# A kernel of attention and gated mixing: the fourth pair of spatial weights loaded earlier, and tiles placed at multiples of 512 bytes

## The chip, the core and the metric

The kernel runs on one core of a Trainium2 chip. A core has five engines that run their own instruction streams and meet through semaphores: TensorE (matrix products, PE in the profile, its weight loads PEld), VectorE (DVE), ScalarE (ACT), GpSimd (POOL) and SyncE (SP), which here only issues transfers. ScalarE and GpSimd issue transfers too. All transfers run on the core's 16 DMA engines. SBUF is the working memory, 128 partitions wide; PSUM holds the results of matrix products.

The metric is device time in microseconds (us) of one execution; lower is better.

## The reference: what is computed

The input x has 2048 tokens of 512 numbers. After a layer norm, two branches read the same xn, and their results are added to x.

```python
x = A_x
xn = _layernorm(x, axis=-1)
return x + _A_ref(xn, A_wqkv, A_wo) + _B_ref(xn, B_w_in, B_w_sp, B_b_sp, B_w_out)
```

Branch A is attention over a sliding window: 32 heads of 16 numbers, each token looks at itself and at the tokens 2, 4, ... 14 before it (8 taps).

```python
logits = jnp.einsum('bhsd,bhswd->bhsw', q, kg) * scale
logits = jnp.where(mask[None, None, :, :], logits, -1000000000.0)
attn = _softmax(logits, axis=-1)
o = jnp.einsum('bhsw,bhswd->bhsd', attn, vg)
```

Branch B is a gated mixing over tokens. z has 1376 columns; the second half is normalised, mixed over all tokens by the 2048 x 2048 matrix w_sp (the spatial weights), and gates the first half.

```python
z = _gelu(jnp.einsum('bsd,df->bsf', x, w_in))
z1 = z[..., :Fh].copy()
z2 = _layernorm(z[..., Fh:], axis=-1)
g = jnp.einsum('ts,bsf->btf', w_sp, z2) + b_sp[None, :, None]
return jnp.einsum('bsf,fd->bsd', z1 * g, w_out)
```

## The kernel before

Tokens are cut into 16 tiles of 128. Everything stays in SBUF: `xnT` holds the normalised tokens transposed, `wts` all input weights (and later the output weights in the same place), `qk0` and `qk1` the queries and keys of the two halves of the tokens, `z2` and `z1` the halves of z, `prod0` and `prod1` products, `vp` the values with a halo of 16 columns, `a_sb` the logits and weights of the attention, `wsp1` and `wsp2` three buffers for the spatial weights. All come from one pool with one buffer each, laid out in SBUF in the order in which they are declared.

The work runs in this order. First the 16 tiles of x are normalised on VectorE, transposed, and multiplied with the weights of z2 (line 225), of queries and keys (265), and then of z1 (225 again). Then come the head sums of the logits (315), the values (280) and the mixing. At the end the output products (423, 437, 450) are added up in PSUM, x is added, and the result is stored.

The mixing is 16 steps M0 to M15 on TensorE (`mix_tile`, line 384), each 32 products of 344 columns: one tile of output tokens against all 16 tiles of z2. Two steps share one load of spatial weights: `load_wsp(n)` (W0 to W7, lines 373 to 377) brings 256 rows of w_sp, transposed on the way, into buffer n modulo 3. W3 thus goes into the buffer of W0, which M0 and M1 read; M6 and M7 use W3. M4 and M5 use W2, M8 and M9 use W4, M10 and M11 use W5. ScalarE moves each result from PSUM to SBUF with the bias (line 387), VectorE multiplies it with z1 (`gate`, g0 to g15, line 392), and SP transposes the product back into `qk0` or `qk1` (line 394).

Beside that, VectorE does the attention. For each half of the tokens (0 and 1): the maximum and its subtraction (x0, x1; lines 325 to 329), ScalarE's exponential (333), the sums (u0, u1; 338 to 340), ScalarE's reciprocal by logarithm and exponential (344, 345), the scaling (c0, c1; 349), and then twelve operations of the taps (a0.0 to a0.11 and a1.0 to a1.11; multiplications line 357, additions 361, the last one 370). Taps from a0.1 on read the halo of V, which GpSimd copies between partitions (lines 286, 287). F0 and F1 are VectorE's last additions of x to the results in PSUM (lines 455, 462); Q0 to Q4 are the output products.

The order of each engine is written out by hand in two lists: `ten` for TensorE with the ScalarE work that belongs to it, `vec` for VectorE. A name in a list emits its instructions, with their transfers on the queue of the engine that issues them. W0, W4 and those after it stand in `ten`. W1, W2 and W3 stand in `vec`, for a reason in the code: `load_wsp` first writes two elements of the buffer on VectorE, so that the transfer follows that memset.

```python
if n in (1, 2, 3):
    V.memset(wsp[n % 3][:, 0, 0:2], 0.0)
SP.dma_start_transpose(wsp[n % 3], B_w_sp[n * 2 * P:(n + 1) * 2 * P, :])
```

The memset of W3 waits until TensorE has finished M1, and SP's transfer waits for the memset. SP issues its transfers in the order of the program: before the change g0's transpose, g1's, W3, g2's, W4, W5.

Of the kernel before, what the change touches and what calls it, by code (L numbers as in the profile page):

```python
# [7 lines left out]
BF16 = mybir.dt.bfloat16  # L8
F32 = mybir.dt.float32
# [4 lines left out]
P = 128  # L14
S = 2048
D = 512
NT = S // P
# [21 lines left out]
def kernel(  # L39
# [22 lines left out]
    sb = ctx.enter_context(tc.tile_pool(name="sb", bufs=1))  # L62
# [17 lines left out]
    b_col = sb.tile([P, NT], F32, name="b_col")  # L80
    stmp = sb.tile([P, 4, GS], F32, name="stmp")

    xnT_r = sb.tile([P, C * S], BF16, name="xnT")
    xnT = xnT_r[:].rearrange("p (c s) -> p c s", c=C)
    op = xnT_r[:].rearrange("p (t d s) -> p t d s", t=2, d=DH)
    wts = sb.tile([P, C * (3 * D + F)], BF16, name="wts")
    w_q, w_k, w_v = [wts[:, C * (FH + n * D):C * (FH + (n + 1) * D)].rearrange("p (k f) -> p k f", k=C) for n in range(3)]

    w_z1 = wts[:, 0:C * FH].rearrange("p (k f) -> p k f", k=C)
# [380 lines left out]
    for i in range(5, NT):  # L470
# [2 lines left out]
    vec = front.split() + """  # L473
        zs0 LW m00 zn0 zn1 zn2 zn3 j00 f00 p00 K m01 d01 m02 d02 zs4 m03 d03 zn4 zn5 zn6 zn7
        p01 p02 zs8 m10 d10 zn8 zn9 zn10 zn11 p03 W1 zs12 m11 zn12 zn13 zn14 zn15 f11 p11 p10 m12 d12
        m13 f13 x0 p13 p12 W2 u0 g0 c0 x1 a0.0 u1 a0.1 g1 W3 c1 a0.2 g2 a0.3 g3
        a0.4 g4 a0.5 g5 a0.6 a0.7 g6 a0.8 g7 a0.9 a0.10 g8 a0.11 g9
        a1.0 a1.1 g10 a1.2 a1.3 g11 a1.4 g12 X1 a1.5 a1.6 g13 a1.7 g14 a1.8 g15 a1.9 a1.10 a1.11 F0 F1
    """.split()
# [278 lines left out]
```

## Time and profile before

| | us |
|---|---|
| median of 3 runs | 201.83 |
| lowest and highest run | 201.72, 201.90 |
| the profiled execution | 201.34 |
| its span (first to last instruction) | 199.6 |
| TensorE busy in it | 194.4 |
| VectorE busy in it | 176.9 |
| ScalarE busy in it | 89.2 |

The profiled execution is one run of its own, 0.49 us below the median; 1.74 us of it lie outside the span. The granted TensorE clock is full speed throughout. In the profile a row of instructions has its line in the kernel, engine, operation, the tiles it writes and reads, and a count; "idle before" is the time in which the engine stood still ahead of them, with what ended it. A row of the timeline begins with its start and its length in us; rows on SPq and POOL that name a DMA show the issue of a transfer, not its length. The chain of waits goes backwards from the last instruction to whatever released each step.

### The profile page before, as it was taken

The page shows a single profiled execution, that of the slowest core. Times are in us where ns is not written, and L with a number is a line of the kernel's source. Part 1 is how long each engine was busy: PE and PEld are TensorE (multiplying, and loading weights), DVE is VectorE, ACT ScalarE, POOL GpSimd, SP SyncE. Part 2 cuts the span into 40 slices and gives each one's busy share as a digit, 9 for nine tenths or more (in the row PEclk, how much of TensorE's full clock was granted, in tenths as well). Part 3 has the DMA queues.
Part 4 walks back from the last instruction along what each step waited for, and adds up shares of the span by engine and source line. Part 5 has one row for each costly group of instructions (what it writes and reads, how often), then busy time and mean ns, then how long its engine had stood idle before and what let it go on. Part 6 is the DMA issues. An engine that isn't in the chain of part 4 may idle for free.

```text
span 199.6 us, 3847 instructions
## 1 busy us (share of the span) xinstructions
PE 194.4 (97%) x1580; PEld 117.9 (59%) x1586; DVE 176.9 (89%) x194; ACT 89.2 (45%) x145; POOL 40.1 (20%) x67
## 2 busy tenths in 40 slices
PE   7999999999999999999999989999999999999993
PEld 2655555655666666666666656666666664444442
DVE  4799789999997999998999999999999999964263
ACT  3868879899888674978531111111112210000000
POOL 4267540138374103000700000011010000000000
PEclk9999999999999999999999999999999999999999
DMA  5999579699959905509808999999999937414033
GB/s 174 295 246 193 106 158 275 120 196 198 198 100 141 208 0 112 107 0 148 124 20 99 234 271 223 231 257 166 255 207 91 267 75 221 84 57 165 0 105 105
DMA packets 64610, 31.09 MB, mean 156 GB/s; under 512 B 53456, under 2 KB 62800, under 8 KB 64464
## 3 DMA queue, kind: packets, MB, share of 16 engines
q1 hardware_dynamic: 59136, 19.24, 48.8%
q0 software_dynamic: 2192, 6.75, 18.0%
q10 hardware_dynamic: 3264, 4.86, 9.5%
q8 instruction: 12, 0.20, 0.4%
q14 instruction: 6, 0.05, 0.1%
HBM read 10.13 MB, written 2.10 MB: 61 GB/s over the span
## 4 chain that ended last, share of the span: by engine, by line
PE 89%; DMA 6%; DVE 3%; issue 1%; POOL 0%
PE mm L384 33%; PE mm L225 18%; PE mm L265 14%; PE mm L280 7%; PE mm L450 7%; PE mm L423 7%; DMA wsp<-in_B_w_sp_dram 5%; PE aux L423 2%; DVE stats L189 1%; DMA z<-in_A_x_dram 1%; PE aux L315 1%; PE mm L437 1%; DVE z L206 1%; DVE mv L190 0%; POOL rstd L197 0%
## 5 line engine op out<-in xcount | busy, mean ns | idle before, releaser
L384 PE MATMUL mm<-z,wsp 128*128 128x344 bf16 x512 | 75.2, 309 | 0.6 <-DMA wsp<-in_B_w_sp_dram 0.6
L384 PEld LDWEIGHTS <-wsp 128*128 128x128 bf16 x512 | 49.9, 98 | 25.7 <-issue 1.3
L225 PE MATMUL mm<-wts,xnT 128*128 128x344 bf16 x256 | 39.5, 309 | 0.1
L387 ACT ACTIVATE qk<-mm,b_col 128x688 bf16<-128x688 f32 x16 | 13.3, 834 | 56.6 <-PE mm L384 52.8
L357 DVE TENSOR_TENSOR prod<-vp,a_sb 128x4096 bf16<-128x4096 bf16 x16 | 36.3, 2285 | 0.0
L225 PEld LDWEIGHTS <-xnT 128*128 128x128 bf16 x256 | 24.7, 98 | 13.7 <-DVE xnT L215 0.4
L301 DVE TENSOR_TENSOR prod<-qk 128x4096 bf16<-128x4096 bf16 (+1 forms) x16 | 31.6, 2020 | 1.2 <-ACT qk L267 1.1
L265 PE MATMUL mm<-xnT,wts 128*128 128x512 bf16 x124 | 28.7, 379 | 0.2
L361 DVE TENSOR_TENSOR prod<-prod,prod 128x8192 bf16<-128x8192 bf16 x6 | 26.5, 4422 | 0.1
L265 PEld LDWEIGHTS <-wts 128*128 128x128 bf16 x128 | 14.6, 114 | 11.9
L267 ACT CAST qk<-mm 128x1024 bf16<-128x1024 f32 x16 | 16.2, 1012 | 4.8 <-PE mm L265 3.8
L280 PE MATMUL mm<-xnT,wts 128*32 128x512 bf16 x256 | 14.5, 379 | 0.0
L450 PE MATMUL mm<-wts,xnT 32*128 32x512 bf16 x192 | 14.3, 374 | 0.0
L423 PE MATMUL mm<-wts,qk 128*128 128x512 bf16 (+1 forms) x63 | 14.0, 370 | 0.2 <-issue 0.2
L257 ACT ACTIVATE z<-mm 128x688 bf16<-128x688 f32 x16 | 11.9, 742 | 4.4 <-PE mm L225 4.4
L423 PEld LDWEIGHTS <-qk 128*128 128x128 bf16 x85 | 8.2, 98 | 9.2 <-issue 0.4
L189 DVE BATCH_NORM_STATS2 stats<-z 128x6 f32<-128x512 bf16 x16 | 11.0, 685 | 2.2 <-DMA z<-in_A_x_dram 2.2
L236 ACT ACTIVATE z<-mm 128x688 bf16<-128x688 f32 x16 | 11.9, 743 | 2.2 <-PE mm L225 2.1
L445 POOL DMA_DIRECT2D qk<-qk x6 | 3.0, 502 | 47.0 <-DMA qk<-z 47.0
L241 ACT ACTIVATE z_junk<-z 128x688 bf16<-128x688 bf16 x16 | 12.3, 771 | 0.0
L280 PEld LDWEIGHTS <-wts 128*32 128x32 bf16 x256 | 9.5, 138 | 4.4
L310 POOL DMA_DIRECT2D prod<-prod x8 | 7.1, 882 | 24.9 <-DVE prod L301 24.9
(97 smaller groups left out, 178.7 us busy)
## 6 DMA issues: line engine op xcount, KB each, us to landing
prod<-prod POOLq DMA_DIRECT2D x8, 512.0 KB, 5.8
wts<-in_A_wo_dram ACTq DMA_DIRECT2D x4, 512.0 KB, 7.0
out_dram<-z SPq DMA_DIRECT2D x9, 128.0 KB, 1.7
z<-in_A_x_dram SPq DMA_DIRECT2D x4, 256.0 KB, 5.1
wts<-in_A_wqkv_dram SPq DMA_DIRECT2D x2, 512.0 KB, 6.6
wsp<-wsp POOLq DMA_DIRECT2D x2, 512.0 KB, 6.2
wsp<-in_A_x_dram ACTq DMA_DIRECT2D x1, 1024.0 KB, 5.8
wsp<-in_A_x_dram SPq DMA_DIRECT2D x1, 1024.0 KB, 6.1
```

The source lines that it names most:

```text
L189: V.bn_stats(stats[:, i, :], xs[:, i, :])
L225: PE.matmul(pz[:, hh, 0:FHALF], xnT[:, kc, i * P:(i + 1) * P], w_z2[:, hh, kc] if part else w_z1[:, kc, hh * FHALF:(hh + 1) * FHALF], star ...
L265: PE.matmul(pq[:, cc, :], w_c[:, kc], xnT[:, kc, t0:t0 + D], start=(kc == 0), stop=(kc == C - 1))
L267: A.copy(qk[b // 2][:, a, 2 * c2:2 * c2 + 2, o:o + D], pq[:])
L280: PE.matmul(pv[32 * g:32 * g + 32, dd, :], w, r, start=(kc == 0), stop=(kc == C - 1), tile_position=(0, 32 * g))
L301: ops.append(lambda ww=ww, k=k, c=c: V.tensor_tensor(pr[:, ww, c], q[:, c], k[:, c], ALU.mult))
L357: return lambda: V.tensor_tensor(dst, vp[:, :, th, off:off + GS], a_sb[:, th, w].unsqueeze(1).broadcast_to([P, DH, GS]), ALU.mult)
L361: return lambda: V.tensor_tensor(dst, dst, x, ALU.add)
L384: PE.matmul(pg[:, hh, 0:FHALF], w[:, k, (j % 2) * P:(j % 2 + 1) * P], z2[:, k, hh * FHALF:(hh + 1) * FHALF], start=(k == 0), stop=(k == NT ...
L387: A.activation(g.rearrange("p (a b) -> p a b", a=2), pg[:, :, 0:FHALF], ACT.Identity, bias=b_col[:, j:j + 1])
L423: PE.matmul(po[:, cols], uT[th][:, m, t0:t0 + P], wout[:, m, cols], start=(start and m == 0), stop=(stop and m == MF - 1))
L450: PE.matmul(po[tiles[g]], op[32 * g:32 * g + 32, th, d, s * P:(s + 1) * P], wo_r[32 * g:32 * g + 32, d, :], start=False, stop=(tiles[g] in ...
```

## The change

Two things are changed. In the list `vec`, W3 moves from behind g1 to behind x1, ahead of the tap a0.0: so its memset stands earlier on VectorE, and its transfer stands ahead of g1's transpose on SP. And two tiles are declared that nothing reads or writes, `pad0` of 64 bytes per partition ahead of `xnT`, `pad1` of 256 ahead of `qk0`. They move all that follows in SBUF, so that `xnT`, `wts`, `qk0`, `wB`, `prod0`, `prod1`, `z2`, `z1`, `vp`, `a_sb`, `wsp1` and `wsp2` begin at multiples of 512 bytes. All engines execute the same instructions as before.

```diff
@@ -80,10 +80,13 @@
     b_col = sb.tile([P, NT], F32, name="b_col")
     stmp = sb.tile([P, 4, GS], F32, name="stmp")
 
+    sb.tile([P, NT], F32, name="pad0")
+
     xnT_r = sb.tile([P, C * S], BF16, name="xnT")
     xnT = xnT_r[:].rearrange("p (c s) -> p c s", c=C)
     op = xnT_r[:].rearrange("p (t d s) -> p t d s", t=2, d=DH)
     wts = sb.tile([P, C * (3 * D + F)], BF16, name="wts")
+    sb.tile([P, 2 * D // 8], BF16, name="pad1")
...
@@ -473,7 +476,7 @@
     vec = front.split() + """
...
-        m13 f13 x0 p13 p12 W2 u0 g0 c0 x1 a0.0 u1 a0.1 g1 W3 c1 a0.2 g2 a0.3 g3
+        m13 f13 x0 p13 p12 W2 u0 g0 c0 x1 W3 a0.0 u1 a0.1 g1 c1 a0.2 g2 a0.3 g3
```

## The prediction

> **What bounds the kernel now.** I read the page's busy shares first, then the chain of waits, then TensorE's own waits, then the timeline around the one wait that is left.
>
> ```profile
> span 199.6 us, 3847 instructions
> PE 194.4 (97%) x1580; PEld 117.9 (59%) x1586; DVE 176.9 (89%) x194; ACT 89.2 (45%) x145; POOL 40.1 (20%) x67
> ```
>
> TensorE is busy for all but 5.2 us of the span, most of that at the two ends. Its waits between 9 and 197 us:
>
> ```profile
> PE mm L384 <- DMA wsp<-in_B_w_sp_dram: 0.6, 1, 0.6
> PE mm L423 <- issue: 0.2, 1, 0.2
> ```
>
> So one data wait is left inside, and the chain of waits says whose it is:
>
> ```profile
> 92.67 13.97 PE mm L384 x96
> 106.65 9.96 DMA wsp<-in_B_w_sp_dram
> 116.61 0.14 issue
> 116.74 8.33 PE mm L384 x56
> ```
>
> The 9.96 us are not lost: the chain follows the load back to its issue, while TensorE went on with M4 and M5. The loss is on the timeline:
>
> ```profile
> 92.61 23.51 PE L384 MATMUL mm<-z,wsp 128*128 128x344 bf16 x160
> 96.35 1.23 DVE L329 TENSOR_TENSOR a_sb<-a_sb,stmp 128x2048 bf16<-128x2048 bf16 x1
> 97.49 0.83 ACT L387 ACTIVATE qk<-mm,b_col 128x688 bf16<-128x688 f32 x1 [2.09 <-PE mm L384]
> 102.48 2.28 DVE L357 TENSOR_TENSOR prod<-vp,a_sb 128x4096 bf16<-128x4096 bf16 x1
> 105.14 0.06 DVE L376 MEMSET wsp<- 128x1 uint32 x1
> 106.65 5.54 SPq L377 DMA_TRANSPOSE wsp<-in_B_w_sp_dram  x1
> 116.74 8.47 PE L384 MATMUL mm<-z,wsp 128*128 128x344 bf16 x57 [0.62 <-DMA wsp<-in_B_w_sp_dram]
> ```
>
> M1 to M5 run without a gap from 92.61 to 116.12; M6 needs W3, which lands at 116.61, and starts at 116.74. The gap is 0.62 us. W3 could have come sooner: its buffer is that of M0 and M1, and M1's eviction begins at 97.49. W3 was held by its memset, which stands behind g1 on VectorE (105.14).
>
> **The move of W3.** On VectorE the memset (0.06) passes six instructions: the tap a0.0, the three sums u1, the tap a0.1 and the gate g1. It now follows L329, which ends at 96.35 + 1.23 = 97.58. It waits for M1, seen finished by ScalarE at 97.49, so VectorE should not stand still. On SP, W3's transpose passes one transfer, g1's. No DMA is added; the queues of POOL and ACT keep their order.
>
> W3 is then issued at about 97.7 (SP is free: g0's transpose went out at 93.72 and one takes 1.2). The eight such loads took 7.6 to 10.0 us to land, so W3 is there between 105.3 and 107.7. M6 can start at 116.12, 8.4 us later at least. The 0.62 us go; the 0.14 of "issue" lie inside them.
>
> Behind W3 on SP stands g1's transpose. SP needs 4.2 to 7.1 us to issue a load, so it is free by 104.8; g1's gate ends at 104.68 + 0.51 = 105.19. No delay. Then g2's transpose (gate ends at 110.03), then W4 at about 111.4 instead of 113.63. It meets the output weights that ACT loads from 111.55, as W3 did before; with W3's slow landing (10.0) it is there at 121.4, and M8 wants it at 116.12 + 2 x 4.67 = 125.5. W5 waits for M5 to leave its buffer (116.1), is issued near 116.5 and lands by 126.5; M10 wants it near 134.8. So no later load becomes the wait.
>
> What starts earlier beside other work: POOL's two copies of V's halo (issued 95.69 and 97.14, 5.3 and 4.1 us to landing) are down at 101.24, and tap a0.1 reads them at 102.48, a slack of 1.24. W2's data began to move 1.5 us after its issue, so W3's begins at 99.2 and overlaps the halo for 2.0 us. From below: no delay, since the busy share of the DMA engines is 0.89 from 98 to 99 us, 0.70 in the next and 0.39 in the one after, so most of the halo is through when W3 comes. From above: the halo behind all of W3 (a rival, below). The nearest row is a small POOL transfer issued beside W3 in this trace: 5.7 us to landing, against 5.1 and 4.8 for the two other such copies of 8 KB, so 0.6 to 0.9 longer. I take that: the halo at 101.9 to 102.1, still in time, cost zero. If this cover goes, each us of stall shifts VectorE by one, and then this slack counts:
>
> ```profile
> DVE wsp L575 <- PE aux L450: 5.3, 1, 5.3
> DVE z L462 <- PE mm L450: 1.5, 1, 1.5
> ```
>
> The second wait is F0 before its first result: 1.48 now, 0.86 when TensorE is 0.62 earlier. F0's four additions end at 179.16 and TensorE takes their banks again at 180.09, 0.93 later. VectorE may therefore lose 0.86 + 0.93 = 1.79 us before TensorE feels it.
>
> **The new addresses.** pad0 (64 bytes) and pad1 (256) shift what follows. From the tiles' sizes, xnT and wts began 448 bytes past a multiple of 512, qk0, wB, prod, z2, z1, vp, a_sb and wsp 192 past; now 0, but for qk1 (256). No instruction is added. For the compute engines the trace prices this: z2 is read at steps of 688 bytes, hence at many offsets, and the 512 matmuls of L384 last 306 to 320 ns; L357 reads vp at a start that moves 4 bytes per tap, 2284 to 2286 ns; ScalarE writes z2 at steps of 1376 bytes (L236) and z1 at 1536 (L257), median 744 for both. Zero, within 14 ns of an instruction.
>
> For DMA the trace has no pair of like transfers at two offsets. Only two places on the path can feel it. One is the first load of x (0.80 to 3.04), which holds the front. The fastest transfer of that size is a store of 1.7 us, so at best 2.24 - 1.7 = 0.5 is gained. The other is the load of tokens 4 and 5, issued at 4.41, 5.0 us; VectorE waits 0.37 us for it, and the copy of transposed tile 3 that TensorE needs next (C3) is queued behind that wait. The slowest of that size took 6.3, so at worst 1.3 is lost; at best 0.04, TensorE's gap there. I take zero, as the engines' rows show no offset that matters, and keep -0.5 and +1.3 for the range.
>
> [...]
>
> **Sum.** The profiled execution took 201.34 us (span 199.6 and 1.74 around it): 201.34 - 0.62 = 200.72. It ran 0.49 below the median of the three runs, 201.83; on that, 201.83 - 0.62 = 201.2.
>
> **Rivals.**
> A second gain, from the addresses. For it: two SBUF ends of transfers lie on the path. Against: nothing in the trace shows an offset's price. Half of the 0.5 bound besides the move: 200.9.
>
> The wait moves on. VectorE, late by 1.8 to 2.4 us for the halo, gives most of it back at Q2; or some later transfer is late. Against: the margins above (8.4, 4.0, 1.79). About 201.7. That the change does not bring W3 forward belongs here: it would need the memset held until g1 anyway, against M1's end at 97.49.
>
> Slower, by the halo. If W3's 1 MB goes ahead of it on the 16 engines, the halo comes with W3, at 97.6 + 7.6 = 105.2 at the earliest; a0.1 stalls 2.7 us, TensorE is late by 2.7 - 1.79 = 0.9 at Q2, net +0.3: 202.1 (with a landing of 10.0, 204.5). It decides from a stall of 2.41. For it: W loads run near 290 GB/s and leave the engines full. Against: the halo starts moving about 1 us ahead of W3, and the 0.6 to 0.9 above. [...]
>
> Slower, by the front: the second load 1.3 us later, 202.5. For it only that bound.
>
> **How the numbers follow.** About 0.2% (0.4 us) is what a measurement of this kernel can tell from no change, so "faster" ends at 201.43. Forecast (201.2): 0.60, of which 0.04 falls short of 201.43 since 0.62 is only 0.22 beyond it. Second gain (200.9): 0.12. Wait moves on (201.7): 0.16. Halo (202.1 and up): 0.08. Front (202.5): 0.04. Faster 0.56 + 0.12 = 0.68; same 0.16 + 0.04 = 0.20; slower 0.12. The range goes down to 200.6 (the move with the whole 0.5 is 200.7, and the runs spread 0.1) and up to 202.1, the halo's nearer price.
>
> **What would show it.** Right: W3's memset near 97.6 and its issue right behind, no wait of L384 on the weights, M6 at 116.1, a0.1 near 102.5, F0's wait near 0.9, every matmul and VectorE row unchanged within 14 ns, x's first load at 2.2. Wrong: a VectorE wait on the vp DMA before a0.1 (halo); a wait at L384 in M8 or M10; Q2 waiting for VectorE; a first load of x well off 2.24, or a start of the L225 work that moved.

## The result

The changed kernel took 200.45 us (median of 6 runs, 200.33 to 200.62). The kernel before, run beside it, had a median of 201.78 (4 of 6 runs); the ratio is 0.9938 (95% interval 0.9923 to 0.9953). That is faster by 0.6%, about twice the 0.3% forecast, and 200.45 lies 0.15 us below the low end of the range. In a later comparison, on another chip, the same two kernels gave 0.997 (0.9952 to 0.9987): the two put the gain at 0.6 and 0.3%. Some executions, of the kernel before above all, take 203 to 217 us; the ratios and the medians leave them out, and "4 of 6" says how many of all are counted.

The page after, its first lines:

```profile
span 198.7 us, 3847 instructions
PE 194.0 (98%) x1580; PEld 117.7 (59%) x1586; DVE 176.9 (89%) x194; ACT 89.3 (45%) x145; POOL 40.1 (20%) x67
```

The profiled execution took 200.43 us, 0.91 less than the one of before. TensorE's waits between 9 and 197 us are now these:

```profile
PE mm L426 <- issue: 0.2, 1, 0.2
```

The wait for the spatial weights is gone. (Three lines were added to the file, so line 384 is now 387, and so on.) The timeline around it, after:

```profile
92.49 34.74 PE L387 MATMUL mm<-z,wsp 128*128 128x344 bf16 x237
96.26 1.23 DVE L332 TENSOR_TENSOR a_sb<-a_sb,stmp 128x2048 bf16<-128x2048 bf16 x1
97.37 0.83 ACT L390 ACTIVATE qk<-mm,b_col 128x688 bf16<-128x688 f32 x1 [2.07 <-PE mm L387]
97.43 0.06 DVE L379 MEMSET wsp<- 128x1 uint32 x1
97.59 6.33 SPq L380 DMA_TRANSPOSE wsp<-in_B_w_sp_dram  x1
102.77 2.29 DVE L360 TENSOR_TENSOR prod<-vp,a_sb 128x4096 bf16<-128x4096 bf16 x1 [0.32 <-DMA vp<-vp]
116.04 0.83 ACT L390 ACTIVATE qk<-mm,b_col 128x688 bf16<-128x688 f32 x1 [3.83 <-PE mm L387]
120.71 0.83 ACT L390 ACTIVATE qk<-mm,b_col 128x688 bf16<-128x688 f32 x1 [3.83 <-PE mm L387]
```

The memset runs at 97.43 and W3 goes out at 97.59. TensorE has one row of 237 products, up to the end of this view, where it had 160, a gap, and the next row. M5's result is evicted at 116.04 and M6's at 120.71, 4.67 us later, which is one step of the mixing.

Where the 0.91 come from, by these evictions. Before, the last two rows of the same kind are

```profile
116.15 0.83 ACT L387 ACTIVATE qk<-mm,b_col 128x688 bf16<-128x688 f32 x1 [3.83 <-DMA wts<-in_B_w_out_dram]
121.60 0.83 ACT L387 ACTIVATE qk<-mm,b_col 128x688 bf16<-128x688 f32 x1 [4.62 <-PE mm L384]
```

M5 came 0.11 us earlier after the change and M6 0.89. So 0.78 were won at M6 and 0.11 in the front; M15's result is 0.89 ahead as well (163.60 and 162.71), and nothing is given back up to the end.

The slack of VectorE, after:

```profile
DVE wsp L578 <- PE aux L453: 5.3, 1, 5.3
DVE z L465 <- PE mm L453: 0.3, 1, 0.3
```

F0 now waits 0.31 us in place of 1.48.

### The profile page after: what moved, and what is told of

It is laid out like the page before. It is cut to its first block, busy times and chain, and to the rows that moved or that the text cites. A ratio compares the mean times of both kernels' runs of the same rounds, so it can differ in the third digit from the quotient of the medians.

```text
span 198.7 us, 3847 instructions
## 1 busy us (share of the span) xinstructions
PE 194.0 (98%) x1580; PEld 117.7 (59%) x1586; DVE 176.9 (89%) x194; ACT 89.3 (45%) x145; POOL 40.1 (20%) x67
## 4 chain that ended last, share of the span: by engine, by line
PE 94%; DVE 3%; DMA 1%; issue 0%; POOL 0%
PE mm L387 38%; PE mm L228 18%; PE mm L268 14%; PE mm L283 7%; PE mm L453 7%; PE mm L426 7%; PE aux L426 2%; DVE stats L192 1%; DMA z<-in_A_x_dram 1%; PE aux L318 1%; PE mm L440 1%; DVE z L209 1%; DVE mv L193 0%; POOL rstd L200 0%; DVE z L586 0%
## 5 line engine op out<-in xcount | busy, mean ns | idle before, releaser
L270 ACT CAST qk<-mm 128x1024 bf16<-128x1024 f32 x16 | 16.2, 1013 | 4.7 <-PE mm L268 3.7
L283 PE MATMUL mm<-xnT,wts 128*32 128x512 bf16 x256 | 14.5, 379 | 0.0
L244 ACT ACTIVATE z_junk<-z 128x688 bf16<-128x688 bf16 x16 | 12.4, 772 | 0.0
```

What stands on the lines that cost most here:

```text
L270: A.copy(qk[b // 2][:, a, 2 * c2:2 * c2 + 2, o:o + D], pq[:])
L283: PE.matmul(pv[32 * g:32 * g + 32, dd, :], w, r, start=(kc == 0), stop=(kc == C - 1), tile_position=(0, 32 * g))
```

## The experiments

A job is a set of kernels run by turns on one chip. The kernel before, over four jobs: 201.5 (32 of 88).

**The move alone**, twice, the second time on the same chip as the whole change.

```diff
-   ... a0.0 u1 a0.1 g1 W3 c1 a0.2 ...
+   ... W3 a0.0 u1 a0.1 g1 c1 a0.2 ...      (no pads)
```

> W3 behind x1, no pads: the move alone. Theory A (two independent gains): the wait at M6 goes and is worth 0.78 us, which is what M6's eviction moved against M5's between the two traces (121.60 - 116.15 = 5.45 before, 120.71 - 116.04 = 4.67 after); the front stays as before (first product of line 265 near 12.3 in the trace, the load of tokens 4 and 5 at 5.0 us). Time 0.996 of before. Theory B (the move is all, and its wait is longer in most executions than in the profiled one): the time is that of the whole change, 0.994. Theory C (the addresses are all: aligned loads land sooner, W3 among them): 0.999 to 1.0. By A and B VectorE still waits about 0.3 us for the halo of V.

> The move without the pads, beside the whole change on the same chip. If the addresses are worth nothing, the undisturbed executions of the two lie within 0.1% of each other, around 200.4, and both have few executions over 203. If they are worth something, this is 0.1 to 0.3% slower and has more of them (3 of 12 in the first run, against 1 of 30 in the kernels with W3 early and pads).

> The whole change again: 200.3 to 200.6, no wait at L384, M5 and M6 evicted 4.67 us apart, and at most one execution of twelve over 203; against the kernel before, whose undisturbed executions lie between 200.2 and 202 as W3's landing takes 7.5 to 10 us or more, a ratio of 0.994 to 0.997.

Measured: 200.61 (9 of 12), ratio 0.9977 (0.9937 to 1.0016); then 200.50 (12 of 12), ratio 0.9963 (0.9941 to 0.9986), beside 200.36 (7 of 8) and 0.997 for the whole change. The trace of the first has no wait at line 384; M5 and M6 are evicted at 116.21 and 120.87, 4.66 apart. The first interval includes 1 and tells little; the second does not, and there the move alone and the whole change have one time within 0.07%, less than the measurement tells. So the move alone gives the gain, as theory B has it. VectorE waited 0.56 us for the halo here, and 0.89 in the second trace of this kernel.

```profile
103.18 2.29 DVE L357 TENSOR_TENSOR prod<-vp,a_sb 128x4096 bf16<-128x4096 bf16 x1 [0.56 <-DMA vp<-vp]
```

**Other addresses, with W3 early.** Once pad0 alone (tiles behind `wts` begin 256 past a multiple of 512), once 32 bytes more (all begin 32 past one, qk1 288).

```diff
-    sb.tile([P, 2 * D // 8], BF16, name="pad1")          (first kernel)
+    sb.tile([P, NT], BF16, name="pad2")                  (second kernel, ahead of xnT)
```

> W3 early, pad0 alone: xnT and wts begin at multiples of 512, the tiles behind them (x, z1, z2, wsp, vp, prod) at 256 past one. [...]

> W3 early, both pads and 32 bytes more ahead of xnT: every tile behind begins 32 bytes past a multiple of 512 (qk1 288). If the addresses of loads matter, the front is at least as slow as with 192 past (tokens 4 and 5 in 5.0 us or more) and the time 0.1 to 0.6 us above the whole change. If they don't, the time is that of the whole change. Matrix products and VectorE rows are to stay within 14 ns either way.

Measured: 200.42 (12 of 12), ratio 0.997 (0.9948 to 0.9992), and 200.46 (11 of 12), ratio 0.997 (0.9949 to 0.9991). They have one time, and it is that of the whole change (200.45 and 200.36), so a start off a multiple of 512 shows no price here. The four loads of 256 KB of x, by the view of transfers, in the two kernels and then in the move alone:

```profile
z<-in_A_x_dram SPq DMA_DIRECT2D x4, 256.0 KB, 4.8
```
```profile
z<-in_A_x_dram SPq DMA_DIRECT2D x4, 256.0 KB, 4.0
```
```profile
z<-in_A_x_dram SPq DMA_DIRECT2D x4, 256.0 KB, 4.1
```

(the last number is the median us to landing). Before it was 5.1, after the change 4.3. At 32 past they land no later than at 0, and without pads sooner than with all of them. The load of tokens 4 and 5, which took 5.0 us in the first trace of before, took 3.3 to 4.1 in the five other traces without pads, and 3.3 to 4.4 in the six with both. The 0.11 of the front is the scatter of single executions, not an address.

**The addresses alone**, twice: W3 back behind g1, both pads.

> Both pads, W3 back behind g1: the addresses alone. Theory A: tokens 4 and 5 land in about 4.3 us in place of 5.0, the front gains 0.1, and the wait at M6 stays within 0.3 us of its 0.62; time 0.998 to 0.9995 of before. Theory B: nothing changes, 1.000. Theory C: W3 lands before M5 ends (in under 9.4 us after its issue near 106.6), no wait at M6, time 0.994 to 0.996.

> The addresses alone, again. By theory D the addresses do nothing: the fast runs spread over the same 200.2 to 202 as the kernel before, ratio 0.998 to 1.002, and a wait at M6 shows when W3 takes over 9.4 us. By theory A (the addresses gain on the front) the ratio is 0.997 to 0.9995 and tokens 4 and 5 land in under 4.4 us. By theory C (the aligned load lands sooner) there is no wait at M6 in any trace.

Measured: one of 6 executions under 203 (200.87), then 6 of 12 (201.40, ratio 0.9951, interval 0.9894 to 1.0008). That interval settles nothing by itself. Both traces are of long executions (209.91 and 212.15 us), and in both M6 does not wait: W3 landed in 7.4 us. The time is lost later. The two further traces of the kernel before are of long executions too:

> The kernel before once more, for another trace of it. Theory D (the wait at M6 is as long as that execution's load of W3 happens to take: 10.0 us in the first trace): the wait at L384 differs from the 0.62 of the first trace, between none (W3 landing in under 9.3 us) and 1.5; span and time follow it one to one, and M5's and M6's evictions lie 4.67 plus that wait plus 0.16 apart. Theory A': the wait is a fixed 0.6 to 0.7 in every undisturbed execution. The time is within 0.3% of before by both.

> The kernel before, one more trace. By theory D the distance of M6's eviction from M5's is 4.67 us when W3 lands within 9.2 us of its issue, and 4.67 + 0.16 + the wait when it lands later; the span moves with it. In the two traces so far W3 took 10.0 (distance 5.45) and 7.5 us (4.67).

The first took 212.13 us in its profiled execution (its timed ones gave 201.84, 5 of 12, ratio 0.9995 with 0.9937 to 1.0052), the second 207.05. Theory D said that M6 waits as long as W3 takes to land, and at M6 that holds in every trace: 10.0 us to landing and a distance of 5.45 between the evictions, 7.4 to 7.5 and 4.67 in four traces. But no time of 200.2 followed. TensorE's waits in the first of these traces:

```profile
PE mm L384 <- DMA wsp<-in_B_w_sp_dram: 8.5, 2, 6.8
```

They stand at M10 (1.7) and M14 (6.8), which use W5 and W7. Reading the issue and the landing of W5 and of the first load of wo (a part of the output weights, on ScalarE's queue behind M6's eviction) in the twelve traces where one goes out behind the other gives a pattern:

| trace | W5 issued | first wo issued | us between | W5 landed in | wo landed in |
|---|---|---|---|---|---|
| before, first | 119.4 | 121.7 | 2.3 | 9.5 | 7.0 |
| before, again (212 us) | 119.7 | 120.7 | 1.0 | 16.6 | 12.8 |
| before, third (207 us) | 119.7 | 121.0 | 1.3 | 16.3 | 14.8 |
| pads alone (210 us) | 119.7 | 120.9 | 1.2 | 16.1 | 14.5 |
| pads alone, again (212 us) | 119.8 | 120.8 | 1.0 | 16.2 | 13.3 |
| move alone | 118.6 | 120.9 | 2.3 | 9.1 | 6.6 |
| move alone, again | 119.2 | 120.9 | 1.7 | 9.8 | 8.0 |
| whole change | 118.4 | 120.8 | 2.4 | 9.5 | 6.9 |
| whole change, again | 118.1 | 120.7 | 2.6 | 9.4 | 6.6 |
| 256 past | 117.9 | 120.6 | 2.7 | 9.1 | 6.2 |
| 32 past | 117.8 | 120.6 | 2.8 | 9.1 | 6.1 |
| W3 behind u1 (below) | 118.2 | 120.8 | 2.6 | 9.3 | 6.5 |

Where wo goes out 1.3 us or less behind W5, both take nearly twice as long. In the first trace of before M6's own wait had pushed wo back by 0.8. So in these five traces the kernel with W3 behind g1 lost either at M6, when W3 came late, or at M10 and M14, when W3 came in time. It does not lose in every execution: four of the 32 under 203 took 200.2 to 200.7 us, as little as the changed kernel, and no trace of such a one is kept.

The distance alone does not decide, though. In the second trace of the move alone the second load of wo goes out 1.2 us behind W6 and the third 0.01 behind W7 (128.92 and 130.13, 139.46 and 139.47); these two land in 5.7 and 4.8 us, W6 in 10.2 and W7 in 12.4, and TensorE does not wait.

The whole change shows neither loss: with W3 gone from between g1 and g2, W4 is issued at 111.7 in place of 113.1 to 113.6 and W5 at 118.4 in place of 119.4 to 119.8. Over all runs 5 of 74 executions with W3 early (in this place or behind u1) took over 203 us; of the kernel before run beside them 56 of 88. The difference stands in each of the four jobs, so it is not one of chips.

**The loads of wo out of the way**, in the kernel before.

```diff
-        ... M6 O0 M7 W6 M8 O1 M9 W7 M10 O2 M11 O3 M12 X0 M13 M14 M15 Q0 ...
+        ... M6 M7 W6 M8 M9 W7 M10 M11 M12 O0 X0 M13 O1 M14 O2 M15 O3 Q0 ...
```

> The kernel before, but with the four loads of wo on ScalarE's queue moved from behind M6, M8, M10 and M11 to behind M12, M13, M14 and M15, where no more spatial weights are loaded. W3 stays behind g1. Theory E (the executions at 203 to 217 us come from the loads of wo meeting those of W5 and W7 on the DMA engines: 12.5 and 16.2 us to landing in such a trace): they are gone, all executions lie between 200.2 and 202, and W4 to W7 land in under 10.5 us. Rival F (they come from outside the kernel): their share stays that of the kernel before, about half.

Measured: 200.35 (5 of 8), ratio 0.9967 (0.9922 to 1.0011), the others 206.4 to 211.9. Theory E said that none would be left, and that is wrong; about as many stay as rival F says, with 8 executions too few to tell. The trace, of a long execution, shows what the edit did and did not do. W5, issued at 120.0, lands in 6.4 us, W6 in 8.5 and W7 in 7.1; those of W5 and W7 are the shortest of all traces, and line 384 does not wait. But now wo is slow: its second and third load take 14.4 and 12.0 us, the fourth is issued only at 176.06, and TensorE's one long wait is for them:

```profile
PE mm L450 <- DMA wts<-in_A_wo_dram: 8.2, 1, 8.2
```

So without wo beside them W5 and W7 land soon, in this one trace; with W3 behind g2 (below), where wo goes out 18 us behind W5, W5 lands in 6.7 too. What lengthens wo itself in its new place is open, and so is whether something outside the kernel takes part.

**W3 later than before.**

```diff
-   ... c0 x1 W3 a0.0 u1 a0.1 g1 c1 a0.2 g2 a0.3 ...
+   ... c0 x1 a0.0 u1 a0.1 g1 c1 a0.2 g2 W3 a0.3 ...
```

> Both pads, W3 later than in the kernel before: behind g2, whose gate ends near 110.0, so that W3 goes out near 110.1 (111.4 if g2's transpose is ahead of it on SP) in place of 106.65. If the landing of W3 sets M6, its eviction slides by 3.5 to 5 us: the wait at M6 is 4 to 5.5 us in place of 0.62, the time 204 to 206.5. If something else takes part in M6's start, the slide is smaller than the shift of the issue.

Measured: 215.7 (all 4 executions, 215.2 to 216.2), ratio 1.0671 (1.0559 to 1.0784). The wait is 13.25, not 4 to 5.5:

```profile
110.80 5.12 PE L387 MATMUL mm<-z,wsp 128*128 128x344 bf16 x34
129.18 13.05 PE L387 MATMUL mm<-z,wsp 128*128 128x344 bf16 x76 [13.25 <-DMA wsp<-in_B_w_sp_dram]
```

The expectation had the queue wrong. At this place of the list W4 and W5 come to stand ahead of W3 on SP, and SP takes 6.71 us to issue W4 (from 111.21) and 4.60 to issue W5 (from 118.02). M5 had left W5's buffer by then, at 115.9, so no buffer held the queue. W3 is issued at 122.72, and M6 starts 6.46 us later. The landing of W3 does set M6; its place on the SP queue sets the landing.

**W3 in between**, behind u1.

```diff
-   ... c0 x1 W3 a0.0 u1 a0.1 g1 ...
+   ... c0 x1 a0.0 u1 W3 a0.1 g1 ...
```

> Both pads, W3 between the change's place and the old one: behind the sums u1, so near 102.5, when the halo of V has landed. Theory: the halo takes 5.3 us as before in place of 7.1, VectorE's wait of 0.3 at a0.1 goes, F0's wait grows from 0.31 to about 0.6, W3 lands by 112.5 and M6 does not wait. Since VectorE has slack, the time is that of the whole change within 0.1%. Rival: the wait at a0.1 is on the path, and this is 0.3 us faster than the whole change.

Measured: 200.43 (12 of 12), ratio 0.9927 (0.9891 to 0.9963). The halo lands in 5.3 us again and a0.1 starts at 102.41 without a wait:

```profile
vp<-vp POOLq DMA_DIRECT2D x1, 96.0 KB, 5.3
vp<-vp POOLq DMA_DIRECT2D x1, 16.0 KB, 4.0
```

The time is that of the whole change (200.45 and 200.36): VectorE's 0.3 us at the halo were not on the path.

## Why the prediction was right, and where not

**The mechanism** was right: W3 behind its memset at 97.43 (forecast 97.6), issued at 97.59 (97.7), 8.9 us to landing (7.6 to 10.0), no wait at M6, no later load in its place. W4 was issued at 111.70 (111.4) and landed in 9.7. W5 came 1.9 later than forecast (118.39 for 116.5), because SP was still issuing W4 (6.58 us from 111.70); it landed at 127.9, 7 us ahead of its use.

**The time** was not: 201.2 was forecast and 200.45 measured. Three sizes make up the 0.76 between 201.21 and 200.45: 0.49 in the base, 0.16 in the gap, and the 0.11 of the front, which is luck.

**The gap at M6** was mis-sized: 0.62 in the sum, 0.78 by the evictions. The step that failed is "201.34 - 0.62", which takes the idle time of the row for the loss. That idle time counts from the end of the last product. A product lasts 309 ns, but in a full stream one starts every 146 ns (4.67 us by 32), so the next would have started 0.16 before that end. The loss is 0.62 + 0.16 = 0.78. The bound of 0.04 for the gap at 10.68 was too small for the same reason.

**The base** was the larger error. The prediction took 0.62 off the median of 201.83, as though the 0.49 us between the profiled execution and the median had another cause and would stay. After the change the profiled execution (200.43) and the median (200.45) agree, so in this job the 0.49 went with the change. That W3's landing, 7.4 to 10.0 us between traces, makes up this 0.49 too is argued: the one trace of before under 203 us cannot show it. Nor is the base fixed: in the later job the executions of before under 203 had a median of 201.05, and the ratio was 0.997, which is the 0.3% that was forecast.

**The addresses** at zero: right, by three other placements: 200.42, 200.46 and 200.36 to 200.45 with 256, 32 and 0 past, 200.50 and 200.61 without pads. A price of 0.1 us is too little for these medians to tell: the two of the whole change differ by 0.09.

**The halo** was taken 0.6 to 0.9 us later, from a POOL copy of 8 KB. It came 1.8 later (5.3 to 7.1 us, and 4.1 to 5.8 for the second copy), and VectorE waited 0.32 for it, which the prediction had named as a sign of being wrong. Of the other traces with W3 in this place one has 0.6 and two have 2.2 and 2.3 (7.5 and 7.7 us to landing). The row of the small copy was a poor one to go by; why, no run tells. That the stall costs nothing held: F0's wait is 1.48 less 0.89 (TensorE earlier) less 0.28 (VectorE later) = 0.31. The rival that makes the kernel slower needed a stall of 2.41, and the largest seen is 0.89.

**The rival that the wait moves on** was not true of the change but of the kernel before, and its first trace could not tell: in four traces with W3 behind g1 and no wait at M6 the loss stood at M10 and M14.

## What to carry to other kernels

A wait for a transfer that shows 0.6 us in one trace is one draw from the scatter of that transfer's landing (7.4 to 10.0 us here); look at the range of its landings and at the margin of the next loads, and expect that more than the wait of that trace may go. Price a gap of a pipelined engine from one result to the next (0.78 us here, where products of 309 ns start every 146), not from the idle time of its row (0.62). Before moving a load in a list, read which other transfers of its queue it comes to stand behind, since here SP issued them one after the other, and two transposing loads ahead, 6.71 and 4.60 us to issue, cost W3 11 us.

## What was not expected of the hardware

A load of wo (512 KB into 32 partitions, ScalarE's queue) issued 1.0 to 1.3 us behind a transposing load of 1 MB on SP's queue took 12.8 to 14.8 us in place of 6.1 to 8.0, and the other 16.1 to 16.6 in place of 9.1 to 9.8. At 1.7 to 2.8 us of distance there was no such loss. No run set the distance by itself, and loads of wo that went out 0.01 and 1.2 us behind W7 and W6 in another trace landed in 4.8 and 5.7 us. So what decides is open.

Behind long waits of TensorE the granted clock was lower, and in two traces the wait cost more than its length. In the trace of 212 us the columns are the stretch, its length, each engine's busy time with its count, then the granted TensorE clock, the busy share of the DMA engines and GB/s:

```profile
132.00:137.00 5.00, 3.26 (x23) 1.99 (x22) 5.00 (x3) 0.83 (x1) 0.00 (x0) 1.00 1.24 190
157.00:162.00 5.00, 0.04 (x1) 0.04 (x2) 1.13 (x1) 0.00 (x0) 0.00 (x0) 0.56 1.01 189
162.00:167.00 5.00, 5.00 (x18) 2.66 (x19) 1.22 (x2) 0.83 (x1) 0.99 (x2) 0.50 0.75 168
```

With the wait of 1.7 us at M10 (first line) the clock was 1.00. With the one of 6.8 us at M14 it was 0.56, and 0.50 while the products ran again: 18 in 5 us, where the stretch from 137 to 142 of the same trace has 36. In the third trace of before M14 starts at 157.96 behind a wait of 3.03 us; the clock was 1.00 from 150 to 155, 0.73 from 157 to 162 and 0.66 from 159 to 164.

```profile
150.00:155.00 5.00, 4.93 (x34) 3.08 (x32) 5.00 (x3) 0.83 (x1) 0.00 (x0) 1.00 1.28 172
157.00:162.00 5.00, 4.04 (x19) 2.37 (x20) 1.68 (x2) 0.83 (x1) 0.99 (x2) 0.73 0.81 172
159.00:164.00 5.00, 5.00 (x25) 2.87 (x23) 2.27 (x2) 0.83 (x1) 0.99 (x2) 0.66 0.83 234
```

There M15's result came 4.87 us late against M13's (14.21 for 9.34). With W3 behind g2 the wait of 13.25 us cost 19.89 - 4.67 = 15.22 between the evictions of M5 and M6 (115.96 and 135.85), 1.8 more than 13.25 and the 0.16 of overlap; the clock was 0.50 there from 122 to 132. So of these four waits the one of 1.74 us shows no lower clock, and those of 3.03, 6.8 and 13.25 us do.
